# A two-layer decode kernel: a new order of work in its groups, and another split of the value caches that stay on the chip between the layers

## The chip, the cores and the metric

The kernel runs on one core of a Trainium2 chip. The metric is the device time of one execution in microseconds (us), the median of several executions. The profile describes one execution of its own.

## The reference, cut to what matters

One token (a row of 640 numbers) goes through two layers that use the same weights and the same caches:

```python
W = 4096                                   # the last 4096 of 32768 cached keys
for layer in range(2):
    # A: 32 heads of 192, a single query
    n = layernorm(x)
    q = (n @ wq).reshape(32, 192)          # wq 640 x 6144
    s = einsum("hd,hkd->hk", q, k_cache[:, -W:]) * 192 ** -0.5
    o = einsum("hk,hkd->hd", softmax(s), v_cache[:, -W:])
    x = x + o.reshape(6144) @ wo           # wo 6144 x 640
    # B: its token mixing is zero for one token
    n = layernorm(x)
    x = x + n + gelu(layernorm(n) @ w3) @ w4   # w3 640 x 1536, w4 1536 x 640
```

All data is bfloat16. The window of one head is 4096 x 192 numbers, 1536 KB of keys (K) and as much of values (V).

## The kernel before, in words

**Cells and the stream.** SBUF holds twelve cells of 1536 KB each (128 partitions by `FREE` = 6144 numbers). A cell takes one head's K or V, one chunk of `wo` (960 KB, the rows of four heads), `w3` or `w4`, or transposed keys. All loads are issued by SyncE (SP) into one DMA queue, in an order that `layer_stream` writes out. A load takes the cell that was given back first (`take` and `give`), so it waits on SP until the last reader of that cell is done, and every load behind it in the stream waits too. At most eight loads are on their way at a time: each has one of eight semaphores, and a load whose semaphore is still out waits for the older load.

**Groups.** The 32 heads are worked in eight groups of four. Layer 0 takes the groups from the last (heads 28 to 31) to the first (heads 0 to 3), layer 1 from the first to the last. In one turn of the loop over groups the kernel weights the values of the current group and makes the scores of the next: `T` transposes half of a K (two of four quarters, DVE, L450), `S` scores that half (PE, L534), `softmax_steps` has seven steps (`part_max` L557, `turn_max` L562, `full_max` L567 and L572, `spread_max` L580 to L586, `turn_p` L591, `swap` L602 to L607, `recip` L614 and L616), and `pv` weights one V (PE, 16 matmuls, L648), gives the V's cell back and turns the result into `o_sb` (DVE, L655). `o_fold` (L662, L663) adds the parts of `o_sb` up. `out_proj` (L676) and `out_row` (L694) multiply by a chunk of `wo`. The engines follow the program's order; no scheduler moves anything.

**What is kept between the layers.** K of heads 0 to 7 is kept, transposed, in eight cells for layer 1. V of head 3 (`VC`) stays in its cell, and `wo` chunk 0 in its own. V of head 2 (`VP`) has 32 blocks of 192 columns: 20 are transposed word by word into PSUM by `v_words(0)` (L637, into `V_bank`) and back in layer 1, and the other 12 are loaded into the room beside `wo` chunk 0. V of head 4 (`VX`) has 24 blocks in two small tiles, `kl` and `kx`; its other 8 blocks are loaded again in layer 1.

**Between the layers.** Layer 0 ends with V 0 to V 3, two chunks of `wo`, `w3` and `w4` in the stream; layer 1 begins with V 0, V 1, K 8, V 4 and K 9. The work in between is one chain: `pv` of V 2 and V 3, `out_proj` of the last group, the sums for the layer norm (L969, L971, read by L974 to L985), `w3` (L1004), GELU, `w4` (L1051), the next layer norm (L396, L398), the query of the first group (`qproj_steps`: `project` L480, `spread` L494, `repeat` L501, `block` L518), and the scores of the kept heads (L534). V 0 of layer 1 waits for `w3`'s cell, V 1 for `w4`'s, and K 8 for the cell of the first kept K, so for the scores of that head. In a line of the profile, L55 is a load in wide form, L156 a load of K or V, L181 a piece of a V, L218 and L220 `w3`, L233 to L239 `w4`. 

**PSUM.** `V_bank` is four banks of 2 KB a partition, `psS` one (scores), `psO` one (`O_ps`), and `psm` two, which all other results of PE use in turn, a whole bank each.

Of the kernel before, what the change touches and what calls it, by code (L numbers as in the profile page):

```python
# [10 lines left out]
F32 = mybir.dt.float32  # L11
# [7 lines left out]
P = 128  # L19
# [40 lines left out]
def kernel(  # L60
# [46 lines left out]
    VC, VP, VX, VW, VN = 3, 2, 4, 20 * Dh // 2, (NKL + NKX) * Dh  # L107
    assert NA * D + FREE - 2 * VW <= FREE
# [20 lines left out]
    psV = ctx.enter_context(tc.tile_pool(name="psV", bufs=1, space=PSUM))  # L129

# [38 lines left out]
    def load_v(layer, h):  # L169
        t = take(("v", layer, h))  # L170
        src = A_v_cache[0, h, s0:Sk, :].rearrange("(p j) d -> p (j d)", p=P)
        cut = (2 * VW,) if h == VP else (FREE - VN, FREE - NKX * Dh) if h == VX else ()
# [3 lines left out]
        for e in cut + (FREE,):  # L176
            kept_v = h == VP or h == VX and i > 0
            if not cut:
                load(t[:], src, layer == 0 or h >= 2)
            elif layer == 0 or not kept_v:  # L180
                nc.sync.dma_start(v_pair(t, h, i, e - i), src[:, i:e])  # L181
            i = e
        return t

    def v_pair(V, h, i, n):

        if h == VP and i >= 2 * VW:
            V, i = loaded["wo", 0, 0], i - 2 * VW + NA * D
        elif h == VX and i >= FREE - NKX * Dh:
            V, i = kx, i - (FREE - NKX * Dh)  # L190
        elif h == VX and i >= FREE - VN:
            V, i = kl, i - (FREE - VN)
        return V[:, i:i + n]
# [53 lines left out]
    def layer_stream(layer):  # L247
# [18 lines left out]
        for gi, cur in enumerate(groups):  # L266
            nxt = list(groups[gi + 1]) if gi + 1 < len(groups) else []
            late = gi + 2 >= len(groups)
            for i, hh in enumerate(cur):
# [7 lines left out]
                if layer == 0 and gi + 1 == len(groups) and i < 2:  # L277
                    seq.append(("wo", layer, groups[gi + i - 1][0] // QH))
# [100 lines left out]
    warm_ps = psm.tile([32, 32], F32, tag="psm")  # L379
# [6 lines left out]
    xT_ps = psm.tile([P, ND], F32, tag="psm")  # L386
# [6 lines left out]
    def ln_center(x, rowsum):  # L393

        mean_ps = psm.tile([P, 1], F32, tag="psm")
# [11 lines left out]
        def total():  # L407
            var_ps = psm.tile([P, 1], F32, tag="psm")
# [46 lines left out]
    def qproj_steps(c, xc, part=None, row=None):  # L455
# [6 lines left out]
        def project():  # L462
            need("wq", 0, ND - 1)
            if row is not None:
                N = QC // 2
                qr_ps = psm.tile([33, N], F32, tag="psm")
# [9 lines left out]
            qT_ps = psm.tile([P, n], F32, tag="psm")  # L476
# [8 lines left out]
        def spread():  # L485
            if row is not None:
                qT_ps = psm.tile([P, n], F32, tag="psm")
# [11 lines left out]
        def repeat():  # L499
            Qrep_ps = psm.tile([P, 4 * n], F32, tag="psm")  # L500
# [50 lines left out]
    def softmax_steps(n, ST_ps, sc, space):  # L551
# [8 lines left out]
        def turn_max():  # L560
            pmT_ps = psm.tile([1, P], F32, tag="psm")
# [16 lines left out]
        def spread_max():  # L578
            nb_ps = psm.tile([P, 1], F32, tag="psm")
# [16 lines left out]
        def swap():  # L596
            ng = NGK // NT
            PT_ps = psm.tile([P, n, NJ4, NGK], F32, tag="psm")
# [7 lines left out]
            l_ps = psm.tile([P, QH], F32, tag="psm")  # L606
# [20 lines left out]
    h_ps = V_bank[:, VW:VW + NF // 2], O_bank[:, 2 * Dh:2 * Dh + NF // 2]  # L627

    def v_words(layer):

        V = need("v", layer, VP)
        step = 512
        for i in range(0, VW, step):
            n = min(step, VW - i)
            a = V[:, 2 * i:2 * (i + n)].bitcast(U32)
            b = V_bank[:, i:i + n].bitcast(U32)
            nc.vector.transpose(b if layer == 0 else a, a if layer == 0 else b)  # L637

    def pv(layer, h, hq, PT, mid=None):
# [13 lines left out]
        else:  # L653
# [453 lines left out]
```

## Time and profile before

| quantity | value |
|---|---|
| runs | 511.27, 511.44, 511.87 us |
| median | 511.44 us |
| the profiled execution: its own time | 511.84 us |
| the profiled execution: span | 509.9 us |
| DMA read | 214.01 MB, 420 GB/s over the span |
| busy: PE, DVE, ACT, POOL | 328.0, 292.0, 48.9, 3.7 us |
| mean granted TensorE clock | 0.681 |

The time of a run covers the span and about 1.9 us around it. The span runs from the first to the last instruction that the profile shows. "Landing" means that the last of the 16 DMA engines has finished a load. A stretch of the trace is named by its start and end in us from the start of the span; layer 0 ends and layer 1 begins at 285 us.

### The profile page before, as it was taken

What the parts mean: (1) busy time and instruction counts of PE and PEld (TensorE: products, weight loads), DVE (VectorE), ACT (ScalarE), POOL (GpSimd) and SP (SyncE); (2) the same over time, 40 slices, a digit from 0 to 9 for tenths busy, and PEclk for the clock granted to TensorE, in tenths of its full rate; (3) what the DMA queues carried; (4) which work ended last, traced back from release to release, by engine and by line L of the source; (5) the groups of instructions that cost most, each with busy time, mean ns of one, the idle gap of its engine ahead of it and who ended that gap; (6) DMA issues with size and microseconds to landing.
All of it is one profiled execution on the core that took longest, in us unless ns stands there. A gap on an engine that the chain in (4) does not pass through costs nothing.

```text
span 509.9 us, 9485 instructions
## 1 busy us (share of the span) xinstructions
PE 328.0 (64%) x4084; PEld 190.0 (37%) x4084; DVE 292.0 (57%) x604; ACT 48.9 (10%) x173; POOL 3.7 (1%) x16
## 2 busy tenths in 40 slices
PE   1057667677586675866665766658656765758685
PEld 0024333333343342533333643435333442434354
DVE  2077557657666656467624244756576566767522
ACT  1000101010010100101010100001010100101111
POOL 2000000000000000000000000000000000000000
PEclk9996666765756667577665585666786577886655
DMA  8999999999999999999999999999999999999996
GB/s 370 432 432 429 438 433 432 429 433 423 419 423 445 432 418 449 428 404 459 429 392 414 377 439 424 435 429 437 429 422 437 432 422 433 426 433 429 419 408 242
DMA packets 12015, 214.63 MB, mean 421 GB/s; under 512 B 2565, under 2 KB 3077, under 8 KB 7429
## 3 DMA queue, kind: packets, MB, share of 16 engines
q1 hardware_dynamic: 11972, 214.02, 98.5%
q8 instruction: 32, 0.52, 0.4%
q14 instruction: 11, 0.08, 0.0%
HBM read 214.01 MB, written 0.00 MB: 420 GB/s over the span
## 4 chain that ended last, share of the span: by engine, by line
DMA 42%; PE 28%; DVE 24%; issue 4%; ACT 1%; SPq 1%; DVEq 0%; ACTq 0%
DMA cell<-in_A_k_cache_dram 24%; DVE cell L450 17%; DMA cell<-in_A_v_cache_dram 14%; PE ST_ps L534 11%; PE O_ps L648 9%; DMA cell<-in_B_w_dram 4%; DVE o_sb L655 2%; PE qr_ps L469 2%; PE nb_ps L580 1%; PE yr_ps L694 1%; DVE words L557 1%; DVE o_sb L591 1%; PE l_ps L607 1%; PE y_ps L1051 1%; PE PT_ps L602 1%
## 5 line engine op out<-in xcount | busy, mean ns | idle before, releaser
L534 PE MATMUL ST_ps<-cell,Qblk 128*16 128x256 bf16 x1536 | 157.0, 364 | 101.6 <-DVE cell L450 69.1
L450 DVE STREAM_TRANSPOSE cell<-cell 128x768 uint32<-128x768 uint32 x224 | 200.3, 943 | 5.8 <-DMA cell<-in_A_k_cache_dram 5.4
L534 PEld LDWEIGHTS <-Qblk 128*16 128x16 bf16 x1536 | 82.8, 108 | 170.8 <-issue 146.9
L648 PE MATMUL O_ps<-cell,PT 128*2 128x384 bf16 x1000 | 103.1, 482 | 9.3 <-DMA cell<-in_A_v_cache_dram 7.4
L655 DVE STREAM_TRANSPOSE o_sb<-O_ps 128x384 f32<-128x384 f32 x64 | 37.2, 581 | 110.4 <-PE O_ps L648 110.3
L648 PEld LDWEIGHTS <-PT 128*2 128x2 bf16 x1024 | 46.1, 102 | 24.7 <-issue 15.7
L591 DVE STREAM_TRANSPOSE o_sb<-o_sb 128x256 bf16<-128x256 bf16 x15 | 6.7, 445 | 33.1 <-ACT o_sb L586 26.1
L663 ACT ACTIVATE words<-oT_ps,words 32x6 bf16<-32x6 f32 x40 | 10.3, 257 | 159.5 <-PE oT_ps L662 148.5
L662 PE MATMUL oT_ps<-o_sb,Lq 128*32 128x6 f32 x160 | 13.8, 195 | 10.4 <-DVE o_sb L655 9.8
L662 PEld LDWEIGHTS oT_ps<-o_sb,Lq 128*32 128x32 f32 x160 | 12.6, 143 | 20.4 <-issue 15.1
L668 ACT ACTIVATE words<-oT_ps,words 32x6 bf16<-32x6 f32 x24 | 6.2, 257 | 111.8 <-PE ST_ps L534 96.3
L480 PE MATMUL qT_ps<-words,wq_sb 128*128 128x1 bf16 x210 | 7.1, 165 | 12.8 <-DMA wq_sb<-in_A_wq_dram 11.9
L694 PE MATMUL yr_ps<-cell,words 128*1 128x320 bf16 x108 | 14.8, 439 | 0.0
L469 PE MATMUL qr_ps<-wq_sb,words 128*1 128x384 bf16 x90 | 14.2, 471 | 0.0
L494 DVE TENSOR_TENSOR o_sb<-qT_ps,words 128x24 bf16<-128x24 f32 (+1 forms) x18 | 3.0, 166 | 18.9 <-PE qT_ps L480 17.1
L480 PEld LDWEIGHTS <-wq_sb 128*128 128x128 bf16 x210 | 6.7, 102 | 14.0 <-DMA wq_sb<-in_A_wq_dram 13.0
L602 PE MATMUL PT_ps<-o_sb,ident 128*32 128x32 bf16 x240 | 6.8, 237 | 7.7 <-DVE o_sb L591 2.6
L607 PE MATMUL l_ps<-o_sb,words 128*128 128x4 f32 x30 | 7.8, 331 | 5.3 <-ACT PT L605 5.3
L602 PEld LDWEIGHTS <-ident 128*32 128x32 bf16 x256 | 5.6, 113 | 14.4 <-issue 14.1
L583 ACT COPY o_sb<-nb_ps 128x1 f32<-128x1 f32 x15 | 2.4, 159 | 88.6 <-PE nb_ps L580 88.6
L667 PE MATMUL oT_ps<-o_sb,Lq 128*32 128x6 f32 x48 | 6.0, 199 | 6.1 <-DVE o_sb L666 6.1
L667 PEld LDWEIGHTS oT_ps<-o_sb,Lq 128*32 128x32 f32 x48 | 5.7, 142 | 10.4 <-issue 9.9
(153 smaller groups left out, 202.0 us busy)
## 6 DMA issues: line engine op xcount, KB each, us to landing
cell<-in_A_k_cache_dram SPq DMA_DIRECT2D x56, 1536.0 KB, 25.6
cell<-in_A_v_cache_dram SPq DMA_DIRECT2D x56, 1536.0 KB, 26.3
cell<-in_A_wo_dram SPq DMA_DIRECT2D x13, 960.0 KB, 23.1
wq_sb<-in_A_wq_dram SPq DMA_DIRECT2D x5, 1536.0 KB, 13.4
cell<-in_A_v_cache_dram SPq DMA_DIRECT2D x6, 768.0 KB, 23.7
cell<-in_B_w_dram SPq DMA_DIRECT2D x1, 1536.0 KB, 11.8
cell<-in_B_w_dram SPq DMA_DIRECT2D x2, 768.0 KB, 10.3
cell<-in_A_wo_dram SPq DMA_DIRECT2D x3, 480.0 KB, 17.0
```

The source lines that it names most:

```text
L450: nc.vector.transpose(Tu, Ku[:, :, q * NY:(q + 1) * NY])
L469: nc.tensor.matmul(qr_ps[32 * i:32 * i + 1, :], lhsT=xc[:, kc:kc + 1], rhs=wq_sb[:, kc, t0 * P + i * N:t0 * P + (i + 1) * N], start=(kc == ...
L480: nc.tensor.matmul(qT_ps[:, tl:tl + 1], lhsT=wq_sb[:, kc, t * P:(t + 1) * P], rhs=xc[:, kc:kc + 1], start=(kc == 0), stop=(kc == ND - 1))
L534: nc.tensor.matmul(ST_ps[r:r + QW, :].rearrange("p (g i) -> p g i", g=ng), lhsT=Q[n], rhs=T4[:, :, f, :, t], start=(hq == 0 and n == 0), s ...
L591: nc.vector.transpose(held["PrT"], held["Pr"])
L602: nc.tensor.matmul(PT_ps[32 * m:32 * (m + 1), :, :, ng * q:ng * (q + 1)], lhsT=Eq[:, q, :], rhs=src[:, m:QW:NM], start=True, stop=True)
L607: nc.tensor.matmul(l_ps[:], lhsT=ones, rhs=held["lh"][:], start=True, stop=True)
L648: nc.tensor.matmul(O_ps[r:r + 2, :], lhsT=PT[:, hq, 2 * i:2 * i + 2], rhs=v_pair(V, h, 2 * i * Dh, 2 * Dh), start=(i < 4), stop=(i >= NB - 4))
L655: nc.vector.transpose(o_sb[:], O_ps.rearrange("p (e a c) -> p e c a", e=2, c=NA))
L662: nc.tensor.matmul(oT_ps[r, :], lhsT=Lq[:], rhs=o_sb[:, e, :, e], start=(e == 0), stop=(e == 1))
L667: nc.tensor.matmul(oT_ps[r, :], lhsT=Lq[:], rhs=o2, start=True, stop=True)
L694: nc.tensor.matmul(yr_ps[32 * i:32 * i + 1, :], lhsT=oT[:, k:k + 1], rhs=wo_t[:, k * D + i * N:k * D + (i + 1) * N], start=(k == 0), stop= ...
```

## The change

**Kept blocks.** V 2 keeps 26 blocks in PSUM, 1984 of its words a partition in `V_bank` and 512 in a bank of `psm` (`v_rest`), and 6 blocks beside `wo` chunk 0. The room beside `wo` chunk 0 then takes the last 6 blocks of V 1 (`VQ`) as well. In layer 1 the load of V 1 brings 26 blocks of V 1 and, in the same cell, 6 blocks of V 4, so that the load of V 4 itself brings 2 blocks (96 KB) and not 8 (384 KB). The cell of V 1 is given back after `pv` of V 4, and not after its own. In layer 0 V 1 is loaded in two pieces.

**One bank for two.** While `v_rest` holds its bank, from `v_words(0)` to `v_words(1)`, all small results use four quarters (128 words each) of the one bank that is left, in turn (`work`, `quarter`, `ps`). Every `psm.tile` becomes `ps`; those lines are left out below.

**The order of work.** In the groups' first part the second half of `T(h0)` comes after `full_max`, and `swap` before `T(h1, 0)`; the first half of the next head's `T` comes ahead of `pv` for the second and third head; layer 0's last but one group takes the order that layer 1's had (`quick`); in layer 0's last group `out_proj` of the group before comes after the second head instead of the first, and `center_y` after the third. The stream of layer 0 ends with V 0, `wo` 0, V 1, `wo` 1, V 2, V 3 instead of V 0, `wo` 1, V 1, `wo` 0, V 2, V 3.

```diff
-    VC, VP, VX, VW, VN = 3, 2, 4, 20 * Dh // 2, (NKL + NKX) * Dh
-    assert NA * D + FREE - 2 * VW <= FREE
+    VC, VP, VX, VQ = 3, 2, 4, 1
+    VW, VB, VN, VR = 26 * Dh // 2, 512, (NKL + NKX) * Dh, 6 * Dh
+    assert NA * D + FREE - 2 * VW + VR <= FREE
     W3C, W4C = FREE // F, FREE // D
...
     psV = ctx.enter_context(tc.tile_pool(name="psV", bufs=1, space=PSUM))
+    quarter = []
+
+    def ps(shape, dtype):
+
+        if quarter:
+            quarter.append(quarter.pop(0))
+            return quarter[-1][0:shape[0], 0:shape[1]]
+        return psm.tile(shape, dtype, tag="psm", name="psm")
+
     ctx.enter_context(tc.manual_schedule(engines={ET.PE, ET.DVE, ET.Activation, ET.SP}))
...
         t = take(("v", layer, h))
         src = A_v_cache[0, h, s0:Sk, :].rearrange("(p j) d -> p (j d)", p=P)
-        cut = (2 * VW,) if h == VP else (FREE - VN, FREE - NKX * Dh) if h == VX else ()
+        x = FREE - VN - layer * VR
+        cut = {VP: (2 * VW,), VX: (x, FREE - NKX * Dh), VQ: (FREE - VR,)}.get(h, ())
         if h in GROUPS[layer][-1][-1 - layer:]:
             cut = FREE // 2,
         i = 0
         for e in cut + (FREE,):
-            kept_v = h == VP or h == VX and i > 0
+            kept_v = h == VP or h in (VX, VQ) and i > 0
             if not cut:
                 load(t[:], src, layer == 0 or h >= 2)
             elif layer == 0 or not kept_v:
                 nc.sync.dma_start(v_pair(t, h, i, e - i), src[:, i:e])
+            elif h == VQ:
+                src = A_v_cache[0, VX, s0:Sk, :].rearrange("(p j) d -> p (j d)", p=P)
+                nc.sync.dma_start(t[:, i:e], src[:, FREE - VN - VR:FREE - VN])
             i = e
         return t
...
         if h == VP and i >= 2 * VW:
             V, i = loaded["wo", 0, 0], i - 2 * VW + NA * D
+        elif h == VQ and i >= FREE - VR:
+            V = loaded["wo", 0, 0]
         elif h == VX and i >= FREE - NKX * Dh:
             V, i = kx, i - (FREE - NKX * Dh)
         elif h == VX and i >= FREE - VN:
             V, i = kl, i - (FREE - VN)
+        elif h == VX and i >= FREE - VN - VR and ("v", 1, VQ) in loaded:
+            V, i = loaded["v", 1, VQ], i + VN
         return V[:, i:i + n]
...
                     seq.append(later.pop())
                 if layer == 0 and gi + 1 == len(groups) and i < 2:
-                    seq.append(("wo", layer, groups[gi + i - 1][0] // QH))
+                    seq.append(("wo", layer, groups[gi - i][0] // QH))
             if gi + 2 < len(groups) and gi >= layer:
                 seq.append(("wo", layer, cur[0] // QH))
...
     O_ps = O_bank[:, 0:2 * Dh]
     V_bank = psV.tile([P, 2048], F32, name="V_ps")
-    h_ps = V_bank[:, VW:VW + NF // 2], O_bank[:, 2 * Dh:2 * Dh + NF // 2]
+    h_ps = V_bank[:, 2048 - NF // 2:], O_bank[:, 2 * Dh:2 * Dh + NF // 2]
+    v_rest = []
     def v_words(layer):
         V = need("v", layer, VP)
-        step = 512
-        for i in range(0, VW, step):
-            n = min(step, VW - i)
+        if layer == 0:
+            v_rest.append(psm.tile([P, VB], F32, tag="psm", name="v_rest"))
+            work = psm.tile([P, 512], F32, tag="psm")
+            quarter.extend(work[:, i:i + P] for i in range(0, 512, P))
+        for i in (*range(0, VW - VB, 512), VW - VB):
+            n = 512 if i == VW - VB else min(512, VW - VB - i)
             a = V[:, 2 * i:2 * (i + n)].bitcast(U32)
-            b = V_bank[:, i:i + n].bitcast(U32)
+            b = (v_rest[0][:, 0:n] if i == VW - VB else V_bank[:, i:i + n]).bitcast(U32)
             nc.vector.transpose(b if layer == 0 else a, a if layer == 0 else b)
+        if layer == 1:
+            quarter.clear()
     def pv(layer, h, hq, PT, mid=None):
...
             loaded["v", 1, h] = V
             cell_of["v", 1, h] = cell_of.pop(("v", 0, h))
-        else:
+        elif (layer, h) != (1, VQ):
             give(("v", layer, h))
+        if (layer, h) == (1, VX):
+            give(("v", 1, VQ))
         nc.vector.transpose(o_sb[:], O_ps.rearrange("p (e a c) -> p e c a", e=2, c=NA))
     def o_fold(h, oT, rl, add=False):
         r = slice(32 * (h % QH), 32 * (h % QH) + 32)
         if not add:
             for e in range(2):
...
             hurry = gi + 2 == len(groups)
             final = gi + 1 == len(groups)
-
-            quick = hurry and layer == 1
+            late = hurry and layer == 1
             ST_n = None
             if nxt:
...
                     T(h0, 0)
                     part_max()
-                    T(h0, 1)
                     S(h0, 0, ST_n, 0)
                     turn_max()
                     full_max()
+                    T(h0, 1)
+                    spread_max()
                     S(h0, 1, ST_n, 0)
-                    spread_max()
                     h1 = nxt[1][1]
                     q = None
...
                         y_ps = out_row(layer, *pending, acc, gi - 1 == rows[0]) if in_row else out_proj(layer, pending)
                     turn_p()
-                    if quick:
-                        y_ps()
-                    T(h1, 0)
                     if q:
                         q[1]()
+                    if in_row:
+                        y_ps()
+                    elif pending is not None:
+                        add_y(y_ps, 2)
+                    pending = None
+                    PT = swap()
+                    T(h1, 0)
+                    if in_row and gi - 1 == rows[-1] and not late:
+                        add_y(turn_row(acc), 2)
+                    if q:
                         q[2]()
-                    if in_row:
-                        if not quick:
-                            y_ps()
-                            if gi - 1 == rows[-1]:
-                                add_y(turn_row(acc), 2)
-                        pending = None
-                    if pending is not None:
-                        add_y(y_ps, 2)
-                        pending = None
-                    PT = swap()
                     T(h1, 1)
                     if q:
...
                 order.insert(0, order.pop(cur.index(VC)))
             for hq, h in order:
-                if quick and hq == 1:
+                if hurry and hq == 1:
                     (q2, h2), (q3, h3) = nxt
                     T(h2, 0)
                     T(h2, 1)
-                elif quick and hq == 2:
+                elif hurry and hq == 2:
                     T(h3, 1)
-                pv(layer, h, hq, PT, steps[3] if quick and hq == 3 else fold)
+                elif nxt and 0 < hq < 3:
+                    T(nxt[0][1], 0)
+                pv(layer, h, hq, PT, steps[3] if late and hq == 3 else fold)
                 if final:
-                    if hq == 0:
+                    if hq == 1 - layer:
                         add_y(out_proj(layer, pending) if layer == 0 else turn_row(acc), 1)
-                    if hq == 1:
+                    if hq == (2, 1)[layer]:
                         center_y()
                     fold = None
...
                     continue
-                if quick and hq == 1:
+                if hurry and hq == 1:
                     S(h2, 0, ST_n, q2)
                     S(h2, 1, ST_n, q2)
                     T(h3, 0)
-                elif quick and hq == 2:
+                elif hurry and hq == 2:
                     S(h3, 0, ST_n, q3)
                     o_fold(h, oT, rl)
                     S(h3, 1, ST_n, q3)
-                    steps = softmax_steps(len(cur), ST_n, sc, kl[:].bitcast(F32))
-                    for step in steps[:3]:
+                    steps = softmax_steps(len(cur), ST_n, sc, kl[:].bitcast(F32) if late else o_words)
+                    for step in steps[:2 + layer]:
                         step()
                     continue
-                elif hurry and hq == 1:
-                    (q2, h2), (q3, h3) = nxt
-                    for half in range(2):
-                        T(h2, half)
-                        S(h2, half, ST_n, q2)
-                    T(h3, 0)
-                    S(h3, 0, ST_n, q3)
-                    T(h3, 1)
-                elif hurry and hq == 2:
-                    S(h3, 1, ST_n, q3)
-                    steps = softmax_steps(len(cur), ST_n, sc, o_words)
-                    steps[0]()
-                    steps[1]()
                 elif nxt and not (hurry and hq == 3):
                     q2, h2 = nxt.pop(0)
...
                 o_fold(h, oT, rl, len(groups) - 4 > gi >= 2 * layer)
                 if hurry and hq == 3:
-                    for step in steps[4 if quick else 2:5]:
+                    for step in steps[4 if late else 2:5]:
                         step()
                     early = steps[5](), steps[6]()
...
```

## The prediction

> **What bounds the kernel now.** The page comes first, its slices and its queue.
>
> ```profile
> span 509.9 us, 9485 instructions
> DMA  8999999999999999999999999999999999999996
> q1 hardware_dynamic: 11972, 214.02, 98.5%
> ```
>
> The 16 DMA engines are busy from the second slice to the last but one. A time saved on another engine is worth nothing unless a transfer starts sooner for it. So I looked for stretches in which the engines wait, with busy times by stretch (the last three columns are granted TensorE clock, DMA share, GB/s).
>
> ```profile
> 40.00:180.00 140.00, 95.17 (x1004) 51.45 (x1007) 90.33 (x169) 14.19 (x46) 0.00 (x0) 0.63 1.00 430
> 270.00:282.00 12.00, 7.62 (x134) 4.83 (x133) 4.94 (x17) 1.38 (x7) 0.00 (x0) 0.50 1.02 416
> 282.00:297.00 15.00, 11.59 (x297) 8.85 (x298) 5.50 (x30) 1.85 (x9) 0.00 (x0) 0.70 0.98 375
> 312.00:490.00 178.00, 121.83 (x1447) 69.19 (x1446) 116.24 (x213) 17.98 (x62) 0.71 (x2) 0.69 1.00 427
> ```
>
> Within both layers the share is 1.00: order alone moves nothing there while loads stay ahead. Only 282 to 297, between the layers, falls to 375 GB/s. What SyncE (SP) issues there, and the chain that its issues wait for, is in the timeline (start, duration; in brackets the idle time before and its releaser).
>
> ```profile
> 263.63 1.77 SPq L181 DMA_DIRECT2D cell<-in_A_v_cache_dram  x4
> 281.70 3.80 SPq L156 DMA_DIRECT2D cell<-in_A_v_cache_dram  x2
> 289.51 0.33 SPq L156 DMA_DIRECT2D cell<-in_A_k_cache_dram  x1
> 291.02 0.33 SPq L181 DMA_DIRECT2D cell<-in_A_v_cache_dram  x1
> ...
> 270.80 2.88 DVE L637 STREAM_TRANSPOSE V_ps<-cell 128x512 uint32<-128x512 uint32 x4 [2.39 <-DMA cell<-in_A_v_cache_dram]
> 275.89 0.81 PE L648 MATMUL O_ps<-cell,PT 128*2 128x384 bf16 x8 [0.73 <-DMA cell<-in_A_v_cache_dram]
> 279.83 0.57 PE L971 MATMUL s_ps<-words 128*128 128x1 f32 x2
> 280.00 0.17 DVE L974 SCALAR_TENSOR_TENSOR words<-s_ps,words 128x5 bf16<-128x5 f32 x1 [0.61 <-PE s_ps L969]
> 283.79 1.36 PE L1051 MATMUL y_ps<-o_sb,cell 128*128 128x1 bf16 x45 [1.79 <-DMA cell<-in_B_w_dram]
> 287.33 0.17 DVE L494 TENSOR_TENSOR o_sb<-qT_ps,words 128x12 bf16<-128x12 f32 x1 [0.56 <-PE qT_ps L480]
> 288.00 1.46 PE L534 MATMUL ST_ps<-cell,Qblk 128*16 128x256 bf16 x24 [0.28 <-DVE Qblk L518]
> ```
>
> The first line is V 2 and V 3 in four pieces, the second V 0 and V 1 of layer 1 (281.70 and 285.18), then K 8 and V 4. By the DMA engines' own landings, `w4` lands at 285.32 on the last engine, V 0 at 289.03, V 1 at 293.25, K 8 at 297.85, V 4 at 298.78, K 9 at 302.40. A 1536 KB load takes that engine 3.64 us, so it idled some 0.07 us ahead of V 0, 0.6 ahead of V 1 and 0.96 ahead of K 8. K 8's issue at 289.51 ends a chain: the first batch of scores ends at 289.46. From there to the end the engine has no gap that a load's issue makes. So what the change does to the bytes, and to the issues from V 2 (263.63) to K 8 (289.51), moves the end one for one.
>
> **1. Bytes.** V 4's own load goes from 384 to 96 KB. It took 0.93 us (297.85 to 298.78). A quarter would be 0.23; the 160 KB piece of `w4` took 0.40 (283.74 to 284.14), and the rows become shorter (768 B), so 0.20 to 0.41, taken as 0.27: -0.66. V 1 in layer 0 comes in two pieces: halves of V 3 took 1.84 each, whole loads 3.64, +0.04. Sum -0.62 (bounds -0.75 to -0.48). V 1 of layer 1 keeps its size.
>
> **2. The kept words.** V 2's first piece is 26 blocks, not 20; the second piece of 12 blocks (576 KB) took 1.38, so the first lands 0.69 later, at 271.47. L637 becomes four of 512 and one of 448 columns; the line's own list has 0.73 for 512 columns and 0.59 for 384, so 0.66 for 448: 3.58, and 0.1 of gaps as before (2.88 for 2.78), some 3.70. DVE then turns V 2's `o_sb`, which holds `O_ps` against V 3's matmuls. Before, V 3's second half waited for its data at 275.89 and ended at 276.70; now DVE is late: 271.47 + 3.70 + 0.54 = 275.71, and two times eight matmuls (0.81 each, with 0.1 between) end near 277.6. That is +0.91 on the chain.
>
> **3. One bank in quarters.** In the changed program's order of instructions, waits stand between results that share the bank. L974 waits for the second sum (L971) and not the first (L969): 279.83 + 0.57 = 280.40 and 0.04 to wake up, against 280.00, +0.44. L494 waits for all 30 query matmuls and not the first 15: the 30 end at 287.69, L494 began at 287.33, +0.40 with the release. Queued behind L494 on DVE is L518, and PE's first scores wait for that. The Trainium skill ("PSUM — Partial Sum Buffer", section "PSUM bank collisions raise a hardware error") says to guard PSUM by bank and quadrant of partitions, not by address, which speaks against four results in one bank; guarded by address the two waits would not be there, and the sum would be 0.84 lower. The program's waits agree with the page. Against this stands 0.16: L1051 waited for `w4`'s landing at 283.74, later than its first operand. So K 8's issue moves by 0.91 + 0.44 + 0.40 - 0.16 = +1.59, V 0's by +1.35, V 1's by some +1.2. Passed on in full, the end moves 1.59 if K 8's first data stays 4.7 us behind its issue (289.51 to 294.21, the start of its 3.64). V 0, with an emptier queue, needed 3.7; a later K 8 has less ahead of it. Below, nothing is paid if the engines' backlog hides it. Bounds 0 to 1.59, taken 1.3, near the full value, as K 8 was already waited for.
>
> **4. Layer 0's last but one group.** Its new order puts the scores of K 3 behind `pv` of V 6, a batch of two halves at 1.46 less what overlapped, so the softmax and `pv` of V 0 come 1.35 to 1.5 later (2.1 at most, with all of K 3's half transposes). V 0's `pv` (262.14, ends 263.59) gives V 2 its cell: V 2's issue goes from 263.63 to about 265.0. The slowest engine is done with the chunk of `wo` ahead at 268.48, the fastest at 265.21. Data 3.5 us behind the issue (between V 0's 3.7 and the 3.3 of a fast engine) reaches the slowest at 268.5, so that it just starves: 0 to 0.75, taken 0.3. V 3 now takes V 1's cell (given at 267.7) where it took that of a `wo` chunk (issue 264.54); its data is due at 272.16, 4.4 us on: 0, and 0.3 if `pv` of V 1 is 1.2 us late. `w3` then waits for `wo` 1's product, issue near 269.5 for data due at 275.8: 0. `w4`, behind L637's longer run, issues near 275 for data due at 280.5: 0. V 7 waits for K 2's transposes, issue 249 for data due over 6 us later: 0.
>
> **5. Layer 1 and the rest.** V 1's cell comes free one head later, so a chunk of `wo` waits for V 2 and K 12 for K 8's last transpose (near 320.9; data due at 323.8): 0, and 0.6 if K 8 runs 3.5 us late. In the other groups, half a `T` is two of 0.94 us; loads of K land 25.6 us after issue (a median), of which 3.64 is their own time, so a shift of 1.9 us is covered more than ten times: 0. The tail, 506.69 (last `w4`) to 509.9, is one chain that the edits do not touch: 0.
>
> Sum: -0.62 + 1.3 + 0.3 = +0.98. The profiled execution's 511.84 gives 512.82; it lies 0.40 above the median, so 512.4 on the median's basis. A measurement of this kernel tells 0.2% (1.0 us) from no change: 510.4 and 512.5 are the borders.
>
> **The rivals.** *Hidden delay.* The engines do not run together: V 1's landing spreads over 1.65 us, V 3's over 2.8. If the later issues find engines with a backlog, 3 and 4 cost nothing and the bytes remain: 511.84 - 0.62 - 0.40 = 510.8. For it: K 8's first engine landed at 296.27, 1.6 ahead of the last. Against it: the slowest engine idled already at K 8. The Trainium skill ("DMA: Bandwidth & Descriptors", section "Specifications") gives about 0.6 us as first-byte latency of a hardware queue, by which this rival would hold; the trace, with 3.7 us from V 0's issue to its data on the last engine, disagrees.
>
> *V 2 starves.* On the slower side: from the point where V 2's issue comes after 264.98 (268.48 - 3.5), every tenth later is an idle tenth on all engines, and V 2's words, V 3 and the whole chain behind go along. At 265.73 (+2.1) that is 0.75 instead of 0.3, and with K 8 paid in full (1.59): 512.4 + 0.45 + 0.29 = 513.1, up to 513.9 if V 3 pays its 0.3 and the bytes only their lower bound. For it: no slack in the estimate of 265.0.
>
> *A faster clock in the chain.* The granted clock was 0.50 from 270 to 282, and a batch of 24 scores takes 1.46 there, 0.86 at 291.22. If the other order of PE's work leaves the clock full between the layers, K 8's issue comes earlier by the difference and by the query's and `w4`'s matmuls, and its 0.96 of idle goes: 511.84 - 0.62 - 0.96 - 0.40 = 509.9. Against it: PE's work in the 20 us before hardly changes.
>
> *The bytes save nothing.* If V 4's short rows cost what 384 KB did, 512.4 + 0.66 = 513.1.
>
> **The numbers.** The forecast (512.4; of its own 511.6 to 513.2) 0.38: each of its terms has a row. Hidden delay 0.26, since half of it is an inference about engines ahead and behind. V 2 starving 0.18, the clock 0.12, the bytes 0.06. Range 510.5 to 513.9: from hidden delay with 0.3 of play to the worst of the starving; the clock's case stays out. Faster by over 0.2%: the clock's 0.12 and 0.08 of hidden delay (its play reaches below 510.4), 0.20. Slower: 0.19 of the forecast (its half above 512.5), and the 0.24 of the two slower rivals, 0.43. The rest, 0.37, within.
>
> **What would show it.** In the changed profile: V 4's load with 96 KB and its landing within 0.4 us of K 8's; L637 five times, ending near 275.2; L974 behind both sums; K 8's issue near 291.1 and its landing near 299.5; V 2's issue near 265.0 and a gap of a few tenths ahead of its data; a share of 1.00 in both layers. K 8 issued before 290, V 2 before 264.5, or a lower share inside a layer would make the forecast wrong.

## The result, and the profile after

The changed kernel took 514.71 us (median of 6 runs, 513.49 to 516.12), the kernel before 511.42 beside it: a ratio of 1.0065, 95% interval 1.0049 to 1.0081, or 3.3 us slower (2.5 to 4.1). The profiled execution took 514.45 us with a span of 512.6. The forecast of 512.4 had the sign; the size is outside its range (510.5 to 513.9).

The page of the changed kernel: the queue moved 0.29 MB less and the span is 2.7 us longer.

```profile
span 512.6 us, 9516 instructions
DMA  8999999999999999999999999999999999999995
q1 hardware_dynamic: 12356, 213.73, 98.2%
```

The stretches of the kernel before, then the same ones of the changed kernel (after the colon the length, then busy times of PE, weight loads, DVE, ACT and POOL; last granted clock, DMA share, GB/s):

```profile
100.00:240.00 140.00, 94.18 (x1047) 53.31 (x1050) 87.94 (x159) 12.83 (x44) 0.00 (x0) 0.66 1.00 430
240.00:260.00 20.00, 13.23 (x147) 7.20 (x140) 12.62 (x22) 1.16 (x5) 0.00 (x0) 0.67 1.01 434
260.00:280.00 20.00, 11.48 (x163) 6.40 (x163) 6.37 (x19) 2.27 (x10) 0.00 (x0) 0.50 0.98 403
280.00:300.00 20.00, 14.73 (x382) 11.40 (x382) 7.55 (x41) 2.42 (x11) 0.00 (x0) 0.73 1.02 398
320.00:335.00 15.00, 10.00 (x124) 5.69 (x123) 9.05 (x18) 0.78 (x3) 0.71 (x2) 0.55 1.03 442
```

```profile
100.00:240.00 140.00, 82.28 (x990) 48.56 (x989) 83.21 (x154) 12.33 (x42) 0.00 (x0) 0.72 1.00 430
240.00:260.00 20.00, 13.67 (x166) 7.68 (x155) 13.74 (x22) 1.30 (x5) 0.00 (x0) 0.67 0.97 410
260.00:280.00 20.00, 10.76 (x162) 6.46 (x162) 6.74 (x17) 2.11 (x8) 0.00 (x0) 0.50 0.97 392
280.00:300.00 20.00, 15.06 (x373) 11.74 (x373) 7.47 (x42) 2.72 (x13) 0.00 (x0) 0.66 1.06 409
320.00:335.00 15.00, 12.29 (x207) 7.94 (x208) 12.37 (x24) 1.40 (x5) 0.71 (x2) 0.74 0.97 393
```

The loss is not where the prediction looked. From 280 to 300, between the layers, the rate rose (398 to 409 GB/s). It fell in two stretches inside the layers that had been full: 240 to 260 (434 to 410) and 320 to 335 (442 to 393).

The share hides part of a stall, since a packet that waits for its first data counts as busy (V 7's first 48 KB packets are recorded with up to 2.6 us, where the median is 1.82). So I counted the lost time from the packets: the length of a stretch, less the work of its packets (each at the median duration of its size) over 16 engines. In us:

```
stretch             before  after   difference
240 to 260           0.00    0.84     +0.84
260 to 280          -0.10    0.51     +0.61
280 to 300           1.66    1.38     -0.28
320 to 335           0.03    1.35     +1.32
500 to the end       4.98    5.70     +0.72
all other             2.04    1.99     -0.05
work of all packets 501.32  500.82    -0.50
sum = span          509.93  512.59    +2.66
```

The two loads behind the new stalls, first in the kernel before (V 7 of layer 0, then K 12 of layer 1), then in the changed kernel, in SP's timeline (start, duration):

```profile
244.10 0.47 SPq L55 DMA_DIRECT2D cell<-in_A_v_cache_dram  x1
311.80 0.47 SPq L55 DMA_DIRECT2D cell<-in_A_k_cache_dram  x1
```

```profile
249.25 0.47 SPq L55 DMA_DIRECT2D cell<-in_A_v_cache_dram  x1
313.77 0.47 SPq L55 DMA_DIRECT2D cell<-in_A_wo_dram  x1
320.81 0.47 SPq L55 DMA_DIRECT2D cell<-in_A_k_cache_dram  x1
```

V 7 is issued 5 us later, K 12 9 us later. A load lands on each of the 16 DMA engines at another time; the "first" and the "last" engine are meant by the order of these landings. They show what the later issues meet. The load ahead of V 7 ended at 249.42 on the first engine and at 252.94 on the last; the first engine did not begin on V 7 before 251.3 (254.91, its landing, less 3.64). The chunk of `wo` ahead of K 12 ended on the first engine at 321.99, and K 12's data began there at 322.95 (326.59 less 3.64); the last engine was at that chunk until 325.52.

The timeline of the changed kernel between V 5 and V 7 shows why V 7 was late (L672 is `pv`, L468 a transpose, L681 the turn of `pv`'s result):

```profile
244.52 1.60 PE L672 MATMUL O_ps<-cell,PT 128*2 128x384 bf16 x14
245.67 3.56 DVE L468 STREAM_TRANSPOSE cell<-cell 128x768 uint32<-128x768 uint32 x4 [1.50 <-DMA cell<-in_A_k_cache_dram]
249.15 0.54 DVE L681 STREAM_TRANSPOSE o_sb<-O_ps 128x384 f32<-128x384 f32 x1
249.25 1.11 SPq L55 DMA_DIRECT2D cell<-in_A_v_cache_dram  x2
```

V 5 was weighted, and its cell free, at 246.1. But in the new order of the program K 2's transposes stand ahead of `pv` of V 5, so K 2's cell is given back first and V 7 takes that one. It waits for K 2's landing and four transposes, to 249.2. V 0 takes the cell of V 5 and is issued right behind: the line's x2.

K 12 is late because V 1's cell is still held: the chunk of `wo` ahead takes the cell of V 2, and K 12 that of K 8, whose last two transposes end at 320.78:

```profile
318.96 1.82 DVE L468 STREAM_TRANSPOSE cell<-cell 128x768 uint32<-128x768 uint32 x2
```

The two loads behind K 12 in the stream are late with it. By the mean landings (less 3.64 a load) the engines stood 0.70 us ahead of K 12, 0.43 ahead of V 12 and 0.20 ahead of K 13.

The chain between the layers, by contrast, moved as worked out (L659 are the word transposes, L985 the first reader of the sums, L512 the first spread of the query):

```profile
272.06 2.94 DVE L659 STREAM_TRANSPOSE V_ps<-cell 128x512 uint32<-128x512 uint32 x4 [1.82 <-DMA cell<-in_A_v_cache_dram]
274.91 0.68 DVE L659 STREAM_TRANSPOSE v_rest<-cell 128x512 uint32<-128x512 uint32 x1
275.50 0.54 DVE L681 STREAM_TRANSPOSE o_sb<-O_ps 128x384 f32<-128x384 f32 x1
280.98 0.57 PE L982 MATMUL work<-words 128*128 128x1 f32 x2
281.58 0.17 DVE L985 SCALAR_TENSOR_TENSOR words<-work,words 128x5 bf16<-128x5 f32 x1 [1.11 <-PE work L982]
289.12 0.17 DVE L512 TENSOR_TENSOR o_sb<-work,words 128x12 bf16<-128x12 f32 x1 [1.03 <-PE work L498]
291.29 0.33 SPq L166 DMA_DIRECT2D cell<-in_A_k_cache_dram  x1
```

K 8 is issued at 291.29 (291.1 forecast), but the data ahead of it was late as well: `w4`'s last piece landed at 286.32 instead of 285.32.

### The profile page after: what moved, and what is told of

It is laid out like the page before. It is cut to its first block, busy times and chain, and to the rows that moved or that the text cites. A ratio compares the mean times of both kernels' runs of the same rounds, so it can differ in the third digit from the quotient of the medians.

```text
span 512.6 us, 9516 instructions
## 1 busy us (share of the span) xinstructions
PE 306.1 (60%) x4084; PEld 184.1 (36%) x4084; DVE 291.8 (57%) x606; ACT 48.9 (10%) x173; POOL 3.7 (1%) x16
## 4 chain that ended last, share of the span: by engine, by line
DMA 68%; PE 15%; DVE 11%; issue 4%; ACT 1%; SPq 1%; DVEq 0%; ACTq 0%
DMA cell<-in_A_k_cache_dram 51%; DMA cell<-in_A_v_cache_dram 11%; DVE cell L468 7%; PE ST_ps L552 7%; DMA cell<-in_B_w_dram 4%; DMA cell<-in_A_wo_dram 2%; PE O_ps L672 2%; DVE o_sb L681 1%; DVE words L575 1%; ACT o_sb L604 1%; PE psm L720 1%; PE psm L702 1%; PE psm L598 1%; PE psm L498 1%; SPq L55 0%
## 5 line engine op out<-in xcount | busy, mean ns | idle before, releaser
L468 DVE STREAM_TRANSPOSE cell<-cell 128x768 uint32<-128x768 uint32 x224 | 201.5, 944 | 41.0 <-DMA cell<-in_A_k_cache_dram 39.1
L672 PE MATMUL O_ps<-cell,PT 128*2 128x384 bf16 x1000 | 82.2, 418 | 8.9 <-DMA cell<-in_A_v_cache_dram 6.0
L681 DVE STREAM_TRANSPOSE o_sb<-O_ps 128x384 f32<-128x384 f32 x64 | 36.1, 565 | 47.1 <-PE O_ps L672 47.1
L672 PEld LDWEIGHTS <-PT 128*2 128x2 bf16 x1024 | 37.3, 93 | 21.6 <-issue 15.4
L512 DVE TENSOR_TENSOR o_sb<-psm,words 128x24 bf16<-128x24 f32 (+1 forms) x15 | 2.7, 180 | 49.7 <-PE psm L508 30.6
L689 ACT ACTIVATE words<-psm,words 32x6 bf16<-32x6 f32 x38 | 9.8, 258 | 149.2 <-PE psm L688 129.8
L688 PE MATMUL psm<-o_sb,Lq 128*32 128x6 f32 x152 | 13.0, 194 | 10.6 <-DVE o_sb L681 10.3
L688 PEld LDWEIGHTS psm<-o_sb,Lq 128*32 128x32 f32 x152 | 10.8, 138 | 20.7 <-issue 13.0
L487 PE MATMUL psm<-wq_sb,words 128*1 128x384 bf16 x90 | 15.9, 516 | 0.0
L694 ACT ACTIVATE words<-psm,words 32x6 bf16<-32x6 f32 x24 | 6.2, 258 | 95.9 <-PE ST_ps L552 55.5
L598 PE MATMUL psm<-words,o_sb 1*128 1x1 f32 x30 | 8.1, 337 | 11.5 <-DVE o_sb L590 11.5
L720 PE MATMUL psm<-cell,words 128*1 128x320 bf16 x108 | 14.7, 435 | 0.0
L598 PEld LDWEIGHTS psm<-words,o_sb 1*128 1x128 f32 x30 | 7.3, 299 | 15.2 <-issue 12.4
L693 PE MATMUL psm<-o_sb,Lq 128*32 128x6 f32 x48 | 5.2, 180 | 8.0 <-DVE o_sb L692 8.0
L625 PE MATMUL psm<-o_sb,words 128*128 128x4 f32 x30 | 7.6, 324 | 3.7 <-ACT PT L623 3.7
```

Of the source, the lines that this page charges most:

```text
L468: nc.vector.transpose(Tu, Ku[:, :, q * NY:(q + 1) * NY])
L487: nc.tensor.matmul(qr_ps[32 * i:32 * i + 1, :], lhsT=xc[:, kc:kc + 1], rhs=wq_sb[:, kc, t0 * P + i * N:t0 * P + (i + 1) * N], start=(kc == ...
L598: nc.tensor.matmul(nb_ps[:], lhsT=held["w"], rhs=one[0:1, :], start=True, stop=True)
L625: nc.tensor.matmul(l_ps[:], lhsT=ones, rhs=held["lh"][:], start=True, stop=True)
L672: nc.tensor.matmul(O_ps[r:r + 2, :], lhsT=PT[:, hq, 2 * i:2 * i + 2], rhs=v_pair(V, h, 2 * i * Dh, 2 * Dh), start=(i < 4), stop=(i >= NB - 4))
L681: nc.vector.transpose(o_sb[:], O_ps.rearrange("p (e a c) -> p e c a", e=2, c=NA))
```

## The experiments

Every kernel ran beside the kernel before, whose median lay between 511.4 and 512.2 us; comparisons go by ratio, where 0.1% is 0.5 us. "Lost" is the time of the table above.

**The parts of the change.** *e1_blocks*: the changed kernel with the old order of work in the groups.

```diff
 # the first part of a turn, as before
-T(h0, 0); part_max(); S(h0, 0, ..); turn_max(); full_max(); T(h0, 1); spread_max(); S(h0, 1, ..)
+T(h0, 0); part_max(); T(h0, 1); S(h0, 0, ..); turn_max(); full_max(); S(h0, 1, ..); spread_max()
 # and: swap() behind T(h1, 0); no T ahead of pv; layer 0's last but one group as before
```

> The kept blocks, the shared bank and layer 0's new order of loads, with the old order of work in the groups. Theory A (the added time is idle of the DMA engines inside the layers, made by the new order of work: about 1.3 us at 240 to 270 and 1.3 us at 320 to 335, and nothing between the layers): 511 to 512 us, idle below 0.3 us at 240 to 270. Theory B (the prediction's: the shared bank and the longer transposes between the layers): 512.5 to 514 us, with the loss at 280 to 300.

Measured: 512.46 us, ratio 1.0013 (1.0001 to 1.0024). Lost: 0.04 at 240 to 260, 0.48 at 260 to 280, 1.42 at 280 to 300, but 1.21 at 320 to 335, which the expectation had not said. That stall belongs to the blocks, not to the order (e2_order, next, has the order without the blocks and 0.02 there).

*e2_order*: the kernel before with the new order and nothing else (the same edit the other way round).

> The kernel before with the new order of work in all groups and nothing else: its blocks, its order of loads at the end of layer 0 and its last group stay. Theory A: 512.3 to 513.0 us, with idle at 240 to 270 as in the changed kernel (1.3 us) and little at 320 to 335, since V 1's cell comes free early. Theory B: 511.2 to 511.8 us.

Measured: 513.76, ratio 1.0031 (1.0016 to 1.0045). Lost: 1.04 at 240 to 260, 0.02 at 320 to 335. The other stall belongs to the order. In time the order costs 1.6 us; its profiled execution (512.32, the fastest of its 12) shows only 0.5 of that against 511.84.

*e3_hurry* and *e4_first* undo one part of the order each in the changed kernel.

```diff
 # e3: only layer 1 takes the quick order in its last but one group
-if hurry and hq == 1:
+if late and hq == 1:
 ...
```

> The changed kernel with layer 0's last but one group in its old order. Theory A: some 1.0 to 1.3 us below the changed kernel's 514.7, so 513.4 to 513.7, the idle at 240 to 270 near that of before (0.15). Theory B: 514.4 to 514.7, unchanged but for V 2's few tenths.

Measured: 514.4, ratio 1.0044 (1.0028 to 1.0060). By the ratios that is 1.1 us below the changed kernel, as expected, but the two intervals overlap. Lost: nothing at 240 to 260, as expected, but 3.11 at 280 to 300, and 1.26 at 320 to 335. The profiled execution (514.68, above the median) shows no gain at all. In it one engine was late with `w4` (287.51, against a mean of 284.67; 286.32 and 285.44 in the changed kernel), and K 8 was issued at 292.18, so that the 3.11 can't be put down to the chain alone.

```diff
 # e4: T(h0, 1) ahead of the maximum and swap() behind T(h1, 0) in all groups
```

> The changed kernel with the old order in the first part of all groups (both halves of the first transposed K ahead of the softmax maximum, the swap behind the next K's first half). Theory A: K 8's transposes end 2 to 3 us earlier, K 12 issues near 318, and the idle at 320 to 335 goes from 1.35 to below 0.5: 513.4 to 513.9 us. Theory B: 514.4 to 514.7 us.

Measured: 514.83, ratio 1.0051 (1.0036 to 1.0065). Lost 0.97 at 320 to 335, a quarter less, and 1.09 at 240 to 260. The expectation was wrong: K 8's transposes now follow each other closely (317.67 to 321.52), but they began 3.2 us later than in the changed kernel, and K 12 was issued at 321.54, not near 318. So this run doesn't show what an earlier K 12 would bring. That the stall does not hang on the order is the result of e1_blocks.

**V 1's cell.** *e6_own* gives it back after its own `pv`; V 4 loads its 8 blocks itself.

```diff
-x = FREE - VN - layer * VR
-cut = {VP: (2 * VW,), VX: (x, FREE - NKX * Dh), VQ: (FREE - VR,)}.get(h, ())
+cut = {VP: (2 * VW,), VX: (FREE - VN, FREE - NKX * Dh), VQ: (FREE - VR,)}.get(h, ())
 ...
-elif (layer, h) != (1, VQ):
+else:
     give(("v", layer, h))
-if (layer, h) == (1, VX):
-    give(("v", 1, VQ))
 # and: V 1's load no longer brings blocks of V 4
```

> The changed kernel with V 1's cell released after its own pv: V 1 loads its 26 blocks only, V 4 loads its 8 blocks (384 KB) into its own cell; the same bytes in all. Theory A (V 1's cell, held for V 4, makes K 12 late: the idle at 320 to 335 in every kernel with it, 1.0 to 1.35 us, and in none without): that idle goes below 0.2 us; up to 0.7 us comes back ahead of K 8, as 288 KB fewer lie ahead of it; sum 0.5 to 1.2 us below the changed kernel, so 1.9 to 2.8 us above the kernel before. Theory C (K 12's wait only takes an idle that would come later): no change, 3.0 to 3.3 above.

Measured: 513.02, ratio 1.0028 (1.0016 to 1.0040); 0.37% less than the changed kernel's ratio, 1.9 us where 0.5 to 1.2 was expected. In its windows the rate at 320 to 335 is back:

```profile
320.00:335.00 15.00, 11.92 (x219) 7.74 (x220) 12.55 (x22) 0.83 (x4) 0.71 (x2) 0.82 1.03 441
```

Lost there: 0.02; at 280 to 300 it is 2.00 instead of 1.38, as the 288 KB of V 4 no longer lie ahead of K 8 (the expectation had up to 0.7 for that). Over all kernels the stall at 320 to 335 is 0.97 to 1.35 in the four that hold V 1's cell, and 0.17 at most in the other fourteen, the kernel before among them.

*e7_blocks_own*: the same edit on e1_blocks.

> The same release of V 1's cell with the old order of work in the groups (the kept blocks alone, without the hold). Theory A: 0.5 to 1.2 us below the 512.46 of the blocks alone, so 0.6 below to 0.1 above the kernel before: the bytes' 0.6 is kept, the longer transposes and the shared bank cost a part of it. Theory C: as the blocks alone, 0.5 to 0.7 above.

Measured: 512.7, ratio 1.0017 (1.0006 to 1.0028), as e1_blocks; the gain that was expected did not come. Lost: 0.05 at 320 to 335 and 2.26 at 280 to 300; the stretch from 500 us on lost 0.54 more. With the old order the hold and its absence cost alike: in these two profiles, what the early release wins at K 12 (1.16 us) it gives back, 0.84 of it ahead of K 8.

**The shared bank.** *e5_quarters*: the kernel before with `work` in quarters between the two `v_words`.

```diff
+if layer == 0:
+    work = psm.tile([P, 512], F32, tag="psm")
+    quarter.extend(work[:, i:i + P] for i in range(0, 512, P))
 # and: every psm.tile becomes ps, and v_words(1) ends with quarter.clear()
```

> The kernel before with one bank in four quarters for the small results between the two v_words, and nothing else. The prediction's step 3: K 8's issue 0.68 us later (0.44 and 0.40 less 0.16), and the end 0.5 to 0.7 us above the kernel before. Hidden delay: no change within 0.2 us.

Measured: 512.31, ratio 1.0008 (1.0000 to 1.0017), 0.4 us. K 8 is issued at 290.38 instead of 289.51, even a little later than the 0.68 of the waits, yet 280 to 300 lost 1.60, no more than the 1.66 before. K 8 even landed earlier (297.34 on the last engine, 297.85 before; 295.74 and 296.27 on the first), with V 1 ahead of it at the same time (293.25 in both). So in these two executions K 8's wait was not set by its issue. The price is between the two expectations and barely clear of nothing.

**Layer 0's last but one group.** *e8_hurry_only*: the kernel before with only that group in the new order.

```diff
-quick = hurry and layer == 1       # and what hangs on it
+if hurry and hq == 1:              # both layers
+    T(h2, 0); T(h2, 1)             # K 2, ahead of pv(V 5)
```

> The kernel before with only layer 0's last but one group in the new order. Theory A: idle of about 0.9 to 1.1 us at 240 to 260 (the V that waits for K 2's transposes issues near 249 instead of 244), part of which the later wait between the layers gives back: 0.5 to 1.3 us above the kernel before. If the first part's order makes the idle: no change.

Measured: 514.75, ratio 1.0046 (1.0030 to 1.0062), 2.4 us (1.5 to 3.2): more than expected, and more than the whole order's 1.0031, though the two intervals overlap. Lost: 1.27 at 240 to 260. V 7's issue in its timeline:

```profile
249.31 0.47 SPq L55 DMA_DIRECT2D cell<-in_A_v_cache_dram  x1
```

*e9_no_hurry*: the rest of the new order on the kernel before, that group as it was.

> The kernel before with the new order of the groups' first part and of the next head's first half, but with layer 0's last but one group in its old order. Theory A (of the new order only that group costs): within 0.3 us of the kernel before, no idle at 240 to 260. Theory D (the first part's order costs as well, by loads later issued everywhere): 0.5 us or more above it.

Measured: 511.85, ratio 0.9999 (0.9989 to 1.0009). The rest of the order costs nothing and brings nothing, as the full queue of the profile before let expect.

*e12_hurry_fifo*: e8_hurry_only with one thing put back, K 2's transposes behind `pv` of V 5, so that V 5's cell is given back ahead of K 2's.

```diff
 (q2, h2), (q3, h3) = nxt
-T(h2, 0)
-T(h2, 1)
 pv(layer, h, hq, PT, fold)
+T(h2, 0)
+T(h2, 1)
 S(h2, 0, ST_n, q2)
```

> The kernel before with layer 0's last but one group in the new order, except that K 2's transposes stay behind the pv of that turn, so that V 7 takes again the cell of the V just weighted and not that of K 2. Theory E (what costs in that group is the order in which cells are given back: V 7's load gets K 2's cell, free 5 us later, and every load behind it waits): the idle at 240 to 260 goes from 1.27 to below 0.2 us, V 7 issues near 244, and of the 2.4 us that the group's order cost 0.5 to 1.2 remain (V 2's later issue, from K 3's scores behind pv). Theory F (the scores of K 3 behind pv are what costs): still 2 us or more above the kernel before.

Measured: 511.76, ratio 0.9995 (0.9985 to 1.0005). The 2.4 us are gone, all of them, where 0.5 to 1.2 was expected to remain, with V 7 issued at

```profile
245.40 0.47 SPq L55 DMA_DIRECT2D cell<-in_A_v_cache_dram  x1
```

and 0.01 us lost at 240 to 260. K 3's scores behind `pv`, which step 4 had priced at 0.3 us, stayed in this kernel: 0.91 us are lost at 260 to 280, and none of it is seen in the time.

**The chain.** *e10_split*: e7_blocks_own with V 2's five transposes split around the turn of its result.

```diff
 nc.vector.transpose(o_sb[:], O_ps.rearrange(..))
+if (layer, h) == (0, VP):
+    v_words(0, 1)          # two of the five; three stand ahead
```

> The kept blocks alone without the hold of V 1's cell (old order of work), with V 2's five word transposes split: three ahead of the turn of V 2's result, two behind it. The prediction's step 2 (the longer transposes hold V 3's second half by 0.9 us): 0.5 to 0.9 us below the same kernel with five in a row, so 0.1 us above to 0.5 below the kernel before, with the idle at 280 to 300 near 1.4. If step 2 costs nothing: as with five in a row, 0.9 above the kernel before.

Measured: 513.05, ratio 1.0024 (1.0014 to 1.0033): no gain. V 3's second half now waits for its data, which lands at 276.50 (276.35 in e7_blocks_own, 275.84 in the kernel before), and K 8 is issued at 290.93 instead of 290.86. The transposes held V 3, but the data would have as well.

*e11_split_new*: the changed kernel with V 1's cell, that group's order and the split mended.

> The changed kernel with its three suspected faults taken out: V 1's cell released after its own pv, layer 0's last but one group in its old order, V 2's transposes split. If these three are the whole cause: within 0.5 us of the kernel before, on either side, and 2.8 or more below the changed kernel. If something else of the new order costs: 1 us or more above the kernel before.

Measured: 512.78, ratio 1.0014 (1.0006 to 1.0023), 0.7 us above the kernel before; 2.6 us less than the changed kernel, where 2.8 or more was expected. Most of the cause is among the three, and the split is none of it (e10_split).

*e13_own_fifo*: the changed kernel with the two cells' turns alone mended (the edits of e6_own and e12_hurry_fifo).

> The changed kernel with both cells' turns mended and all else kept: V 1's cell released after its own pv, and K 2's transposes behind the pv in layer 0's last but one group. Theories A and E: no idle at 240 to 260 nor at 320 to 335; what is left is the chain between the layers and V 2's issue: 0.5 to 1.3 us above the kernel before, some 2.2 below the changed kernel. If the two are not the cause: 2 us or more above the kernel before.

Measured: 512.49, ratio 1.0008 (0.9999 to 1.0017). Of the changed kernel's 0.65%, 0.57 go with two edits that alter the order in which cells are given back, and beside that only the load in which 288 KB of V 4 come. The two stretches of the changed kernel's stalls lost 0.06 and 0.04 us:

```profile
240.00:260.00 20.00, 13.76 (x179) 7.48 (x176) 13.50 (x21) 1.04 (x4) 0.00 (x0) 0.67 0.98 420
320.00:335.00 15.00, 12.27 (x198) 8.34 (x199) 12.36 (x24) 1.60 (x6) 0.71 (x2) 0.67 1.04 443
```

**K 8's wait.** Three kernels shorten the chain ahead of K 8: e14_query (on e13_own_fifo) and e15_query_before (on e12_hurry_fifo) move half of the query behind the first scores, e16_query_sum moves the second sum of the norm as well.

```diff
 qa[0]()
-qb[0]()
 for step in qa[1:]:
     step()
-qb[1]()
 ...
 if (hq, half) == (0, layer):
+    qb[0]()
+    qb[1]()
     qb[2]()
```

> The changed kernel with both cells' turns mended, and in layer 1 the second half of the first group's query (15 matmuls and its steps) moved behind the first scores, for which K 8's load waits. By the trace of the changed kernel: L512 waits no longer for 30 but for 15 query matmuls (0.4 us) and PE has 15 fewer ahead of the scores (0.47 us), so K 8 issues up to 0.9 us earlier. If the wait of K 8 is what is left between the layers: 0.4 to 0.9 us below the same kernel without the move, so 0.5 below to 0.1 above the kernel before. If other loads set that stretch: no change, 0.4 above.

> The same move of the query's second half on the blocks of the kernel before (with the new group order and K 2's transposes behind pv, which was even with the kernel before). K 8 issues about 0.5 us earlier; if its wait counts: 0.3 to 0.5 us below the kernel before; if not, even.

> The first of these with the second sum of the norm (L982) also moved behind the first 24 w3 matmuls, so that L985 waits only for the first sum: the price of the shared bank at that place, 0.44 us in the prediction. If it counts: 0.2 to 0.4 us below that kernel. If not, even with it.

Measured: 513.53, ratio 1.0032 (1.0020 to 1.0044); 512.62, 1.0014 (0.9999 to 1.0029); 513.63, 1.0031 (1.0020 to 1.0043). The move of the query misses with both sets of blocks, and the second sum brings nothing on top. e14_query issues K 8 at 290.70 instead of 291.28, but V 4 at 293.00 instead of 292.79 and K 9 at 294.90 instead of 294.70, behind the moved matmuls, and 280 to 300 lost 2.44 instead of 1.64. Shortening the wait for one load by putting the work ahead of the next two is no gain; that it is a loss of 1.2 us is not explained by 0.2 us of issue.

No version beat the kernel before: e9_no_hurry and e12_hurry_fifo are even with it, and e13_own_fifo, with 0.29 MB less to read, is within 0.9 us above.

## Why the prediction was wrong, step by step

**Bytes (step 1)**: right. -0.62 forecast, -0.50 of packet work measured; V 4's piece landed 0.26 us behind K 8 (300.11 and 300.37; 0.27 forecast).

**Kept words and shared bank (steps 2 and 3)**: right as a chain, wrong as a price. Word transposes to 275.59 and V 2's turn to 276.04 (275.17 and 275.71 forecast, with V 2 0.56 later than reckoned), L985 behind the second sum, K 8 at 291.29 (291.1). But 280 to 300 lost 0.28 less than before, where +1.3 was taken. The step let the end move with K 8's issue, on the condition that its first data stays 4.7 us behind. That condition failed: counted like the 4.7, on the last engine, it was 5.2 in the changed kernel and 3.3 in e5_quarters, and on the first engine 3.1 in the kernel before, 2.1 in the changed kernel and 1.7 in e5_quarters, whose K 8 was issued 0.87 later and landed 0.5 earlier. What else holds K 8 in the kernel before was not found. V 7's stall is not why the price stayed away, for e1_blocks has no such stall, issued K 8 at 291.09 and lost 1.42 there, 0.24 less than before. The bank alone cost 0.4 us, at most 0.9 (e5_quarters; 0.68 by its waits). The Trainium skill's rule to guard PSUM by bank and quadrant of partitions ("PSUM — Partial Sum Buffer", section "PSUM bank collisions raise a hardware error") agrees with what L985 waited for, the sum in the neighbouring quarter of the bank.

**Layer 0's last but one group (step 4)**: the term that failed first. V 2's issue was right (264.41; 265.0 forecast). But of V 7 the step said "issue 249 for data due over 6 us later: 0". Its issue was right (249.25), the due time was not: 252.94 on the last engine, 3.7 us on, and 249.42 on the first, at once. The trace of before had it so (253.00 and 249.72). The stall is 0.84 us in the changed kernel. By itself this turn of cells cost 2.4 us (e8_hurry_only, gone in e12_hurry_fifo), and in the changed kernel with V 1's cell mended some 1.0 (e6_own against e13_own_fifo, by the ratios).

**Layer 1 (step 5)**: the term that failed second. "K 12 for K 8's last transpose (near 320.9; data due at 323.8): 0". K 12 was issued at 320.81, as said. The lead of 2.9 us passed for cover, but it was taken on the last engine; the first was done at 321.99, 1.2 us on. The stretch lost 1.32 us more, with the two loads behind. In time V 1's cell cost 1.9 us in the new order (e6_own) and nothing in the old one (e7_blocks_own against e1_blocks).

**What the two terms share.** Both followed the last of the 16 engines alone, and in the changed kernel these are 0.6 to 4.4 us apart. On the last engine both loads were in time: V 7 landed there 3.63 us behind the load ahead of it and K 12 3.61, no more than the 3.64 that a load takes. The engines that were ahead stood still. V 7's due time was misread besides. That the lost time of the engines ahead counts is shown by the runs in which it is gone. How it reaches the end is not: behind the first stall the last engine was no later than before (V 0 of layer 0 landed at 260.20; 260.27 before), behind the second it was 1.9 us later (K 13: 336.60 and 334.68), as much as the mean. The table adds up to the span by its making, and doesn't say which of its rows hangs on which.

**The sign was luck.** Of the forecast's +0.98, 1.3 came from a price that was hardly paid; most of the loss came from two terms put at 0 (0.57% of 0.65, e13_own_fifo).

**Hidden delay.** This rival (510.8) was near the truth between the layers, where the later issues cost little, and had no room for the stalls inside them. Against it the prediction held 3.7 us from the issue of layer 1's V 0 to its data, but the last engine was at `w4` until 285.32, and V 0's data began there at 285.39; on the first engine it was 2.05 (287.39 less 3.64 less 281.70). From V 7's issue to the first engine's start on it passed 2.0, and 2.1 from K 12's. The Trainium skill's 0.6 us of first-byte latency ("DMA: Bandwidth & Descriptors", section "Specifications") is again not what these rows show.

**The other rivals.** V 2 starved a little (0.61 more lost at 260 to 280; 0.3 was taken), but e12_hurry_fifo lost 0.91 there without being slower. The granted clock between the layers was 0.66 against 0.73, so the clock's case did not come. The bytes were saved.

**Open.** The stretch from 500 us to the end lost 0.72 more in the changed kernel (4.6 to 6.4 over all kernels). Of that 0.72, 0.63 is how far the last engine lies behind the mean landing of the last `w4` piece (2.24 us, 1.61 before); what sets that was not tried. Nor is it settled why V 1's cell costs nothing in the old order, or why e14_query is slower than e13_own_fifo.

## What to carry to other kernels

Where loads take buffers in turn, the order in which the program gives the buffers back decides what a load waits for, not the time at which some buffer is free: a step moved ahead of another can hand the next load a buffer that is free 3 us later, with every load behind it in the queue. So list for each moved step which load takes its buffer, and compare its issue with the time at which the first of the DMA engines runs dry, with the issue-to-data time of the trace on top. And before a load's issue is taken for what a stretch waits for, move that issue and see whether the landing moves: K 8, issued 0.87 us later, landed 0.5 earlier (e5_quarters).

## What the runs showed of the hardware

The 16 DMA engines of one queue ran up to 4 us apart (landings of the last `w4` piece in the changed kernel: 505.06 on the first, 509.19 on the last). From an issue to the first engine's data (its landing less 3.64) 2.0 to 2.1 us passed at V 7 and K 12; at K 8 of layer 1 it was 3.1 in the kernel before and 1.7 in e5_quarters, so it is no constant. A packet's wait for its first data stands in its recorded time: up to 2.6 us for the first 48 KB packets of V 7 against 1.82.
